# Moving the second rank's weight loads, its split and the first rank's stores behind the first units' turned rows, and ending the last table at the fifteenth step

## The chip, the cores and the metric

The kernel runs on one core of a Trainium2 chip. The metric is the device time in microseconds (us) of one execution. Engines are named as in the profile: PE (matrix multiply), DVE (vector), ACT (scalar), POOL (GpSimd, which here issues the indirect DMAs) and SP (which issues most of the other DMAs).

## The reference

The first part is an attention in which columns, not tokens, are normalised: for each of 4 batches a 256x256 matrix `softmax(kn^T qn)` is formed from 5056 tokens and applied to `v`. The second part is a top-1 mixture of 8 experts over all 20224 rows of its result:

```
logits = x @ w_gate;  e_idx = argmax(logits);  gate_w = softmax(logits)[e_idx]
eom = sigmoid(x @ w_output_gate)
for e in range(8):
    mask = e_idx == e
    h = maximum(x[mask] @ w1[e], 0)        # 256 -> 1024
    ye = h @ w2[e]                         # 1024 -> 256
    out[mask] = gate_w[mask] * eom[mask, e] * ye
```

## The kernel before, in words

The attention of each batch is a gram stage (`gram`), a softmax and a mix (`mix`). While a batch is mixed, its tokens are routed: each token's row is scattered to a slot of its expert in DRAM (`xs_d`) by indirect DMAs of POOL, eight for each group of 1024 tokens (L731). After the last group two more indirect DMAs fill the slots behind the last token of each region (L772).

The expert part works in units of 256 tokens of one expert (`blocks`). Experts are ordered by the number of their tokens; the place in this order is the rank. For a unit, its rows are read from `xs_d` into `xg` (L1013), scaled and cut into two f16 halves `xr` by ACT (L1065) and DVE (L1066), and turned by two pairs of DMA transposes into `xt` (L1070, issued by SP; two instructions to a unit). `h_part` runs four times a unit, each time 12 matmuls (L1091 to L1093) into a PSUM tile that ACT (L1095) and DVE (L1096) turn into the halves of `hb`. `y_part` multiplies `hb` by the second weights (L1117 on the high half, L1119 on the low one) and ACT (L1125) and DVE (L1126) write `yo`, which POOL scatters to the output (L1132). u0, u1, ... below are these units in order.

Weights. For each rank the raw weights come in two halves (the first and the second matrix). `load_raw` reads them on SP: for the second rank in two pieces each into `vall`, a buffer of the attention (L339), for later ranks in one 1 MB transfer into `raw` (L341). `split` squares them on ACT for a scale (L404), sums that by a small matmul (L410), and cuts them into f16 halves on ACT (L431) and DVE (L432). `keep` stores the halves to the scratch `wsc` in DRAM (L439); the first rank's `keep` calls are put into a list `held` instead, two of them with two 512 KB stores each. Units u0 to u6 use the first rank's halves where they lie in `wbuf`; from u7 on POOL fetches each unit's weights from `wsc` (L984).

Two checkpoints make tables: the early one covers the first ten units, the last one (`final`, L792 to L882 on DVE) all others. POOL reads a mark behind the scatters (L744), and the indices of later units wait for it.

What sets the order: `_beside` advances one generator and feeds others at a rate: `run` yields the expert work step by step, `preps` the weight work (`prep`), `tail` the last steps of the last mix. `pause(n)` yields n times. Each engine executes its instructions in the order that results, after a scheduler that keeps program order among dependent work and has some freedom elsewhere; `behind("SP")` puts a DMA behind the last main instruction of SP. SP issues its DMAs in order, and an SP instruction that waits (a transpose for its `xr`, say) holds all that follow on SP.

Of the kernel before, what the change touches and what calls it, by code (L numbers as in the profile page):

```python
# [26 lines left out]
def _beside(main, *others):  # L27

    due = [0.0 for _ in others]
    for _ in main:  # L30
        for i, (gen, rate) in enumerate(others):
            due[i] += rate
            while due[i] >= 1.0:
                due[i] -= 1.0
                next(gen, None)
# [3 lines left out]
def tile_colnorm_attention_then_top1_moe(  # L39
# [57 lines left out]
    for u in range(NUNIT):  # L97
# [6 lines left out]
        else:  # L104
            pair, half = divmod(u - MID, 2)
# [46 lines left out]
    PRATE = 1  # L152
    ALONE = 18
    LATE = 12
    MWAIT = 12
    BRATE = 0.7
    SOON, SRATE = 20, 1.0
    WRATE = 0.45
    WAITW = 1
    RWAIT = 3  # L160
    PIECES = "0 0 01 00 0 1 01 1 00"
    PWAIT = 2
    SMALL = 9
    VAFTER = 6
    AHEADW = 2
# [99 lines left out]
    @contextmanager  # L265
    def behind(*engines):
        with ExitStack() as held_back:
            for e in engines:
                if e in last:
                    held_back.enter_context(tc.issue_after(last[e]))  # L270
            yield

    def in_turn(gen, *engines):
        while True:
            with behind(*engines):
                try:
                    next(gen)
                except StopIteration:
                    return
            yield  # L280

    def pause(n):
        for _ in range(n):
            yield
# [38 lines left out]
    def load_raw(r, half, tag):  # L323
        if tag == "v":
            raw = [v_rows() for i in range(2)]
        else:
            if tag == "st":
                raw = wk.tile([P, R, CW], F32, tag="st", name=f"raw{r}_{half}", bufs=STB)
            else:
                raw = wide(f"raw{r}_{half}")  # L330
            whole = raw.rearrange("p r w -> p (r w)")[:, :HW1]
            raw = [whole[:, i * HW1 // 2 : (i + 1) * HW1 // 2] for i in range(2)]
        row = nc.values_load(
            ri[0:1, r : r + 1], engines=[mybir.EngineType.SP], min_val=0, max_val=(E - 1) * P,
            skip_runtime_bounds_check_because="rows of the weights of an expert",
        )
        if tag == "v":
            for i, a in enumerate(raw):
                nc.sync.dma_start(a, wraw[half][bass.ds(row, P), i * HW1 // 2 : (i + 1) * HW1 // 2])  # L339
        else:  # L340
            nc.sync.dma_start(whole, wraw[half][bass.ds(row, P), :])  # L341
        return raw

    held = []
    parts_of = {}

    def prep(first, end, tag):
        todo = []
        for r in range(first, end):
            for half in range(2):  # L350
                with behind("SP"):
                    raw = load_raw(r, half, "v" if r == first else tag)
                todo.append(lambda raw=raw, half=half, r=r: in_turn(split(raw, half, r), "ACT", "DVE", "PE"))
                yield
                if len(todo) > AHEADW:
                    if r == first + 1:
                        yield from pause(PWAIT)
                    yield from todo.pop(0)()
        for f in todo:
            yield from f()  # L360
# [3 lines left out]
    def prep_first():  # L364

        raws = []
        for half in range(2):
            raws.append(load_raw(0, half, "raw"))
            yield
        yield from pause(RWAIT)  # L370
        parts = [in_turn(split(raw, half, 0), "ACT", "DVE", "PE") for half, raw in enumerate(raws)]
        for step in PIECES.split():
            for half in step:
                next(parts[int(half)], None)
            yield
        first_done.append(0)
        while not mixed:
            yield
        for part in parts:
            yield from part  # L380
# [215 lines left out]
    def finish(gen):  # L596
        for _ in gen or ():
            pass
# [544 lines left out]
    def blocks(a, z):  # L1143

        got = dict.fromkeys(("x", "prep"), a)
        todo = sorted(range(max(a, FIRST[1]), z), key=lambda u: (asked_at(u), u))

        def adv(stage, step, n):
            for u in range(got[stage], min(n, len(units), z)):
                step(u)  # L1150
                got[stage] = u + 1

        g = a
        while g <= z:
            while g < z and g + 1 > len(units):
                yield
            while todo and asked_at(todo[0]) <= g:
                u = todo.pop(0)
                assert u < len(units)
                fetch_w(0, u)  # L1160
                fetch_w(1, u)
            adv("x", fetch_x, got["prep"] + XAHEAD - (got["x"] in BY_POOL))
            if g > a + 1:
                store(g - 2)
            if g == a:
                yield
            if g == 0:
                yield
            adv("prep", prepare, g + 1)
            if g == 0:  # L1170
                yield from pause(XWAIT)
            if g < z:
                hb = wide("hb").rearrange("p r w -> p (r w)")[:, :HW1]
                units[g]["h"] = hb.bitcast(F16).rearrange("p (a f m) -> p a f m", a=2, f=FC)
            for fp, steps in enumerate(ORDER):
                for kind, part in steps:
                    if kind == "h" and g < z:
                        h_part(g, part)
                    if kind == "y" and g > a:
                        y_part(g - 1, part)  # L1180
                adv("prep", prepare, min(g + 1 + XP, got["prep"] + (fp % 2 or g == a)))
                yield
            g += 1
        store(z - 1)
# [12 lines left out]
    run = blocks(0, NUNIT - TAIL)  # L1197
# [4 lines left out]
    preps = prep_first()  # L1202
    tail = mix(B - 1)
    for i in range(ALONE):
# [5 lines left out]
        for _ in range(PRATE):  # L1210
            next(preps, None)
    mixed.append(True)
    rest, preps = preps, prep(1, E, "st")
    for _ in range(AHEADW):
        next(preps)
    _beside((next(tail) for _ in range(2)), (run, BRATE), (rest, 1))
    finish(rest)
    finish(early)
    _beside(tail, (run, BRATE))
    for keep in held:  # L1220
        keep()
    final = checkpoint(True)
    next(final)
    _beside((next(run) for _ in range(MWAIT)), (preps, SRATE))
    finish(final)
    _beside((next(run) for _ in range(SOON - MWAIT)), (preps, SRATE))
    _beside(run, (preps, WRATE))
# [38 lines left out]
```

## Time and profile before

| what | value |
|---|---|
| median of 3 runs | 1264.32 us (1263.8 to 1269.23) |
| profiled execution | 1267.87 us, span 1266.2 us |
| mean granted PE clock of that execution | 0.975 |
| PE busy | 1194.1 us (94% of the span) |
| DVE, ACT, POOL busy | 767.9, 619.9, 566.5 us |

The profiled execution is one single execution; its time is its span and 1.67 us around it, and it lies 3.55 us above the median. All views below are of this execution. A timeline row gives the start, the time from start to end (for xN rows of the whole group), engine, line, operation, output and inputs, and in brackets how long the engine stood idle before it and what released it. PE rows overlap: a matmul of 256 columns lasts 0.27 us but the next one starts 0.11 us later at the full clock.

### The profile page before, as it was taken

How to read it: one execution, taken by the hardware profiler on the slowest of the kernel's cores; microseconds unless marked ns; L12 is line 12 of the kernel's file. 1: busy time of each engine (PE TensorE's matmuls, PEld its weight loads, DVE VectorE, ACT ScalarE, POOL GpSimd, SP SyncE). 2: the span in 40 equal slices, each digit the busy share in tenths (PEclk: the TensorE clock that was granted, in tenths of full speed). 3: DMA queues.
4: the chain of work that ended last, by engine and by line, in shares of the span. 5: the costliest groups of instructions: out<-in, count | busy, mean ns of one | idle time of the engine just before them, and what ended most of it. 6: DMA issues, size and time to landing. Idle time of an engine off the chain costs nothing. (4 is left out here: it accounts for less than half of the span.)

```text
span 1266.2 us, 25393 instructions
## 1 busy us (share of the span) xinstructions
PE 1194.1 (94%) x9138; PEld 950.0 (75%) x9138; DVE 767.9 (61%) x2292; ACT 619.9 (49%) x1233; POOL 566.5 (45%) x561
## 2 busy tenths in 40 slices
PE   9999899997748799999999999999999999999997
PEld 8888888897746477777777777777777777777775
DVE  7667547554546767575767666755555655555552
ACT  6577448545544365555555455543333333333442
POOL 0003653654445424445454544454445554444442
PEclk9999999898878999999999999999999999999999
DMA  9976776654537998465556554983334533347852
GB/s 324 329 245 222 235 242 224 233 182 154 191 124 178 239 276 221 136 146 142 144 148 142 145 140 111 247 186 70 73 71 136 143 73 78 78 114 209 193 178 62
DMA packets 175161, 214.68 MB, mean 170 GB/s; under 512 B 120200, under 2 KB 123790, under 8 KB 169528
## 3 DMA queue, kind: packets, MB, share of 16 engines
q1 hardware_dynamic: 130600, 126.58, 36.7%
q0 software_dynamic: 43312, 86.01, 23.7%
q8 instruction: 74, 1.21, 0.4%
q14 instruction: 55, 0.45, 0.2%
q10 hardware_dynamic: 1120, 0.42, 0.1%
HBM read 275.55 MB, written 61.41 MB: 266 GB/s over the span
## 5 line engine op out<-in xcount | busy, mean ns | idle before, releaser
L1096 DVE SCALAR_TENSOR_TENSOR hb<-h_ps,hb 128x512 f16<-128x512 f32 (+1 forms) x360 | 226.2, 634 | 239.3 <-ACT hb L1095 183.6
L1095 ACT ACTIVATE hb<-h_ps 128x512 f16<-128x512 f32 (+1 forms) x360 | 194.7, 549 | 274.6 <-PE h_ps L1093 177.9
L1132 POOL DMA_INDIRECT out_dram<-yo,b_id x162 | 168.2, 1038 | 244.3 <-DVE p2e L294 143.8
L731 POOL DMA_INDIRECT xs_d<-st,r_si x160 | 167.8, 1049 | 239.1 <-ACT st L656 150.5
L1117 PE MATMUL y_ps<-wbuf,hb 128*128 128x512 f16 x784 | 266.4, 380 | 1.3 <-DVE yo L1126 0.6
L1091 PE MATMUL h_ps<-xt,wbuf 128*128 128x256 f16 (+1 forms) x928 | 227.8, 258 | 4.8 <-DMA xt<-xr 3.2
L1092 PE MATMUL h_ps<-xt,wbuf 128*128 128x256 f16 (+1 forms) x928 | 227.8, 258 | 1.5 <-issue 1.5
L1093 PE MATMUL h_ps<-xt,wbuf 128*128 128x256 f16 (+1 forms) x928 | 227.6, 257 | 1.0 <-issue 1.0
L1119 PE MATMUL y_ps<-wbuf,hb 128*128 128x256 f16 x784 | 213.1, 274 | 1.9 <-issue 0.9
L1117 PEld LDWEIGHTS <-hb 128*128 128x128 f16 x1296 | 126.8, 98 | 115.3 <-issue 1.9
L1117 PE MATMUL y_ps<-vall,hb 128*128 128x512 f16 x512 | 173.2, 379 | 1.4 <-issue 0.9
L505 PE MATMUL s_ps<-qk 128*128 128x256 f32 x640 | 150.1, 384 | 0.1
L1119 PEld LDWEIGHTS <-hb 128*128 128x128 f16 x1296 | 127.0, 98 | 26.7 <-issue 7.0
L1119 PE MATMUL y_ps<-vall,hb 128*128 128x256 f16 x512 | 139.6, 273 | 1.1 <-issue 0.8
L1091 PE MATMUL h_ps<-xt,vall 128*128 128x256 f16 x512 | 139.5, 272 | 0.7 <-issue 0.7
L1093 PE MATMUL h_ps<-xt,vall 128*128 128x256 f16 x512 | 139.5, 273 | 0.0
L1092 PE MATMUL h_ps<-xt,vall 128*128 128x256 f16 x512 | 139.5, 273 | 0.0
L653 PE MATMUL x_ps<-ah,vh 128*128 128x272 f32 x320 | 105.6, 332 | 32.2 <-ACT st L656 17.3
L984 POOL DMA_INDIRECT wbuf<-wsc,wi x102 | 107.3, 1052 | 57.6 <-PE h_ps L1093 26.3
L505 PEld LDWEIGHTS s_ps<-qk 128*128 128x128 f32 x640 | 118.9, 192 | 15.8 <-issue 1.4
L1065 ACT ACTIVATE xr<-xg,b_sx 128x256 f16<-128x256 f32 x162 | 74.3, 501 | 111.7 <-DVE b_sx L295 61.2
L1091 PEld LDWEIGHTS <-wbuf 128*128 128x128 f16 x928 | 91.3, 98 | 32.3 <-issue 6.0
(212 smaller groups left out, 2057.9 us busy)
## 6 DMA issues: line engine op xcount, KB each, us to landing
qk<-in_q_dram SPq DMA_DIRECT2D x75, 256.0 KB
qk<-in_k_dram SPq DMA_DIRECT2D x75, 256.0 KB
vall<-in_v_dram SPq DMA_DIRECT2D x32, 512.0 KB
raw<-in_moe_w_dram SPq DMA_DIRECT2D x14, 1024.0 KB
xg<-xs_d SPq DMA_DIRECT2D x30, 272.0 KB
wsc<-whi SPq DMA_DIRECT2D x14, 512.0 KB
wsc<-wlo SPq DMA_DIRECT2D x14, 512.0 KB
vall<-in_v_dram SPq DMA_DIRECT2D x8, 480.0 KB
```

The lines of the kernel that those rows point to most:

```text
L505: nc.tensor.matmul(s_ps[:, c, :], kt[:, 1, t, c * P : (c + 1) * P], qt[:, 0, t, :], start=st == 0 and t0 == 0 and t == 0 and c == 0 and n ...
L653: nc.tensor.matmul(x_ps[:, :CW], vh[:, c, tsl], ah[:, c, :], start=c == 0, stop=False)
L731: ins = nc.gpsimd.indirect_dma_start(out=xs_d[:, :], out_offset=bass.IndirectOffsetOnAxis(ap=si[:np_, t : t + 1], axis=0), in_=st[:np_, t, ...
L984: nc.gpsimd.indirect_dma_start(out=weight(half, u), out_offset=None, in_=wsc[half][:end, :], in_offset=bass.IndirectOffsetOnAxis(ap=units[ ...
L1091: nc.tensor.matmul(hp, w1s[:, 0, c, fs], xh, start=fi == 0 and c == 0, stop=False, **KWM)
L1092: nc.tensor.matmul(hp, w1s[:, 0, c, fs], xl, start=False, stop=False, **KWM)
L1093: main(PE=nc.tensor.matmul(hp, w1s[:, 1, c, fs], xh, start=False, stop=fin, **KWM))
L1095: main(ACT=nc.scalar.activation(hh, h_ps[:, :, :w], AF.Relu))
L1096: ins = nc.vector.scalar_tensor_tensor(out=hb[:, 1, 2 * fp : 2 * fp + 2, :w], in0=h_ps[:, :, :w], scalar=0.0, in1=hh, op0=ALU.max, op1=ALU ...
L1117: nc.tensor.matmul(y_ps, hb[:, 0, f, tsl], w2s[:, :, f, :], start=f == 0, stop=False, **KWM)
L1119: PE=nc.tensor.matmul(y_ps[:, 0, :], hb[:, 1, f, tsl], w2s[:, 0, f, :], start=False, stop=f == FC - 1, **KWM)
L1132: ins = nc.gpsimd.indirect_dma_start(out=out[:, :], out_offset=bass.IndirectOffsetOnAxis(ap=un["id"][:, t : t + 1], axis=0), in_=un["yo"][ ...
```

## The change

Four constants and two places of code. `MWAIT`, the number of `run` steps over which the last table's work is spread before it is finished, goes from 12 to 15. `PWAIT`, the pause before the second rank's first split, goes from 2 to 4, and that pause with the split stands ahead of the load of the third rank's first half instead of behind it. The two `next(preps)`, which issue the second rank's raw loads, stand behind the last steps of the mix instead of ahead of them. The first rank's stores are issued one pair after `KWAIT` = 6 steps of `run` and the other after 3 more, instead of both ahead of the last table.

```
-    MWAIT = 12
+    MWAIT = 15
...
-    PWAIT = 2
+    PWAIT = 4
+    KWAIT = 6
...
             for half in range(2):
+                if (r, half) == (first + 1, 0):
+                    yield from pause(PWAIT)
+                    yield from todo.pop(0)()
                 with behind("SP"):
                     raw = load_raw(r, half, "v" if r == first else tag)
...
                 if len(todo) > AHEADW:
-                    if r == first + 1:
-                        yield from pause(PWAIT)
                     yield from todo.pop(0)()
...
     rest, preps = preps, prep(1, E, "st")
-    for _ in range(AHEADW):
-        next(preps)
     _beside((next(tail) for _ in range(2)), (run, BRATE), (rest, 1))
     finish(rest)
     finish(early)
     _beside(tail, (run, BRATE))
-    for keep in held:
-        keep()
+    for _ in range(AHEADW):
+        next(preps)
     final = checkpoint(True)
     next(final)
-    _beside((next(run) for _ in range(MWAIT)), (preps, SRATE))
+    for n in (KWAIT, KWAIT // 2, MWAIT - KWAIT - KWAIT // 2):
+        _beside((next(run) for _ in range(n)), (preps, SRATE))
+        if held:
+            held.pop(0)()
     finish(final)
```

On SP, at the first units, the order before is this. `xr_4679` holds u2 and u3, `xr_5052` u4 and u5, `xr_5334` u6 (x4 is two units' transposes):

```order
237 L1070 DMA_TRANSPOSE xt<-xr_4679 128x4x128 x4
238 L439 DMA wsc_85<-wbuf_184 128x2048 x2
239 L439 DMA wsc_86<-wbuf_185 128x2048 x2
240 L1009 TENSOR_LOAD gi
241 L1013 ISA
242 L1013 DMA xg<-xs_d 128x544
243 L1009 TENSOR_LOAD gi
244 L1013 ISA
245 L1013 DMA xg<-xs_d 128x544
246 L333 TENSOR_LOAD ri
247 L341 ISA
248 L341 DMA raw_0_5009<-in_moe_w_dram 128x2048
```

```order
249 L1070 DMA_TRANSPOSE xt<-xr_5052 128x4x128 x4
250 L333 TENSOR_LOAD ri
251 L341 ISA
252 L341 DMA raw_1_5291<-in_moe_w_dram 128x2048
253 L439 DMA wsc_85<-whi 128x2048
254 L439 DMA wsc_85<-wlo 128x2048
255 L1070 DMA_TRANSPOSE xt<-xr_5334 128x4x128 x2
```

Of the changed kernel the same place on SP (its lines are two higher; `xr_5043` holds u4 and u5, `xr_5322` u6):

```order
244 L1072 DMA_TRANSPOSE xt<-xr_5043 128x4x128 x4
245 L441 DMA wsc_85<-wbuf_184 128x2048 x2
246 L441 DMA wsc_86<-wbuf_185 128x2048 x2
247 L1072 DMA_TRANSPOSE xt<-xr_5322 128x4x128 x2
248 L441 DMA wsc_85<-whi 128x2048
249 L441 DMA wsc_85<-wlo 128x2048
250 L334 TENSOR_LOAD ri
251 L342 ISA
252 L342 DMA raw_0_5332<-in_moe_w_dram 128x2048
253 L334 TENSOR_LOAD ri
254 L342 ISA
255 L342 DMA raw_1_5361<-in_moe_w_dram 128x2048
```

The first rank's four stores stand behind the transposes of u4 and u5 instead of ahead of them, and the third rank's two raw loads behind u6's transposes and the second rank's first two stores. Ahead of the rows shown the four loads to `vall` have moved from ahead of the transposes of u2 and u3 to behind them, and all four reads of `xg` stand between them and the transposes of u4.

On DVE, before, the last table's first long operations stand ahead of the first `hb` of u2 (the first L1096 here):

```order
666 L1066 SCALAR_TENSOR_TENSOR xr_5052<-xg,b_sx,xr_5052 128x256 x2
667 L828 TENSOR_TENSOR tb_pr<-tb_bm,ef 128x496
668 L828 TENSOR_TENSOR tb_pr<-tb_bm,tb_r_4888 128x496
669 L793 TENSOR_SCALAR tb_ni<-tb_n 128x8
670 L829 TENSOR_REDUCE tb_res<-tb_pr 128x62
671 L1096 SCALAR_TENSOR_TENSOR hb<-h_ps,hb 128x512
672 L829 TENSOR_REDUCE tb_res<-tb_pr 128x62
```

In the changed kernel they stand behind it (the first L1098 here):

```order
665 L1068 SCALAR_TENSOR_TENSOR xr_5043<-xg,b_sx,xr_5043 128x256
666 L794 TENSOR_TENSOR tb_n<-rcr,done 128x8
667 L807 TENSOR_TENSOR tb_r_4921<-done,eor 128x8
668 L1098 SCALAR_TENSOR_TENSOR hb<-h_ps,hb 128x512
669 L830 TENSOR_TENSOR tb_pr<-tb_bm,ef 128x496
670 L830 TENSOR_TENSOR tb_pr<-tb_bm,tb_r_4884 128x496
671 L795 TENSOR_SCALAR tb_ni<-tb_n 128x8
672 L1098 SCALAR_TENSOR_TENSOR hb<-h_ps,hb 128x512
```

Three operations of 496 columns (two L828, one L829) have moved behind the first `hb` of u2. On ACT one of the two squarings of the second rank's first half (L404) has moved in the same way. From about u9 on the two orders are alike but for small swaps, and the numbers of instructions are the same.

## Rows read from the trace of the kernel before

**Rows 1.** Busy time of the engines in four stretches of the span (length; then PE, PEld, DVE, ACT, POOL busy with instruction counts; the granted PE clock; the DMA engines' share; GB/s).

```profile
280.00:400.00 120.00, 84.74 (x616) 77.29 (x615) 60.23 (x259) 58.18 (x144) 60.44 (x62) 0.83 0.47 151
400.00:460.00 60.00, 50.21 (x348) 34.12 (x346) 42.59 (x164) 28.61 (x52) 23.53 (x23) 0.94 1.11 249
460.00:1266.20 806.20, 795.66 (x6509) 598.92 (x6506) 489.52 (x1468) 364.23 (x721) 382.49 (x368) 1.00 0.55 138
```

**Rows 2.** The same view by tens of us, at the stretches the prediction speaks of.

```profile
350.00:360.00 10.00, 1.96 (x11) 1.65 (x11) 1.43 (x8) 0.39 (x1) 7.22 (x8) 0.70 0.50 158
360.00:370.00 10.00, 2.49 (x11) 2.49 (x12) 2.17 (x6) 3.08 (x6) 3.48 (x4) 0.50 0.54 177
...
410.00:420.00 10.00, 6.78 (x42) 3.82 (x40) 6.41 (x25) 0.91 (x2) 8.01 (x7) 0.94 1.08 352
420.00:430.00 10.00, 8.65 (x50) 4.74 (x48) 6.69 (x33) 4.24 (x9) 4.25 (x5) 0.89 1.29 185
430.00:440.00 10.00, 7.98 (x66) 5.94 (x63) 9.68 (x33) 7.71 (x11) 0.15 (x1) 1.00 1.17 156
440.00:450.00 10.00, 8.27 (x53) 5.88 (x54) 6.38 (x20) 4.63 (x10) 2.55 (x3) 0.83 1.05 283
```

**Rows 3.** The waits of PE from 400 to 460 us (what waited for what: us in total, times, longest).

```profile
PE h_ps L1091 <- DMA xt<-xr: 2.8, 1, 2.8
PE h_ps L1091 <- issue: 1.6, 2, 1.1
PE h_ps L1092 <- issue: 1.5, 2, 1.2
PE y_ps L1119 <- DVE hb L1096: 0.8, 1, 0.8
PE y_ps L1117 <- DVE yo L1126: 0.6, 1, 0.6
```

**Rows 4.** PE's timeline around u4's first matmul.

```profile
438.56 0.38 PE L1117 MATMUL y_ps<-wbuf,hb 128*128 128x512 f16 x1
441.73 0.27 PE L1091 MATMUL h_ps<-xt,wbuf 128*128 128x256 f16 x1 [2.79 <-DMA xt<-xr]
441.83 0.27 PE L1092 MATMUL h_ps<-xt,wbuf 128*128 128x256 f16 x1
...
442.84 0.42 PE L1092 MATMUL h_ps<-xt,wbuf 128*128 128x256 f16 x1
443.06 0.42 PE L1093 MATMUL h_ps<-xt,wbuf 128*128 128x256 f16 x1
...
446.23 0.27 PE L1092 MATMUL h_ps<-xt,wbuf 128*128 128x256 f16 x1
```

**Rows 5.** SP's timeline of DMA issues.

```profile
400.03 0.70 SPq L339 DMA_DIRECT2D vall<-in_moe_w_dram  x1
...
403.44 5.85 SPq L1070 DMA_TRANSPOSE xt<-xr  x4
409.33 3.71 SPq L439 DMA_DIRECT2D wsc<-wbuf  x4
414.62 2.00 SPq L1013 DMA_DIRECT2D xg<-xs_d  x2
418.97 0.62 SPq L341 DMA_DIRECT2D raw<-in_moe_w_dram  x1
419.62 15.40 SPq L1070 DMA_TRANSPOSE xt<-xr  x4
435.79 0.35 SPq L341 DMA_DIRECT2D raw<-in_moe_w_dram  x1
...
445.29 2.52 SPq L1070 DMA_TRANSPOSE xt<-xr  x2
```

**Rows 6.** The queue that carries SP's DMAs, by packets, MB and share of 16 engines' time, from 405 to 410 us and then from 425 to 430 us.

```profile
q1 hardware_dynamic: 1791, 0.91, 133.2%
...
q1 hardware_dynamic: 264, 0.20, 106.6%
```

**Rows 7.** DVE's timeline at the rows the prediction speaks of.

```profile
414.40 0.66 DVE L828 TENSOR_TENSOR tb_pr<-tb_bm,ef 128x496 f32<-128x496 f32 x1
414.99 0.66 DVE L828 TENSOR_TENSOR tb_pr<-tb_bm,tb_r 128x496 f32<-128x496 f32 x1
...
415.94 0.67 DVE L829 TENSOR_REDUCE tb_res<-tb_pr 128x62 f32<-128x496 f32 x1 [0.20 <-DVE tb_ni L793]
...
423.31 0.69 DVE L1096 SCALAR_TENSOR_TENSOR hb<-h_ps,hb 128x512 f16<-128x512 f32 x1 [6.70 <-issue]
...
438.33 1.29 DVE L1096 SCALAR_TENSOR_TENSOR hb<-h_ps,hb 128x512 f16<-128x512 f32 x2
```

**Rows 8.** ACT's timeline at the rows the prediction speaks of.

```profile
408.39 1.05 ACT L404 ACTIVATE whi<-vall 128x1024 f16<-128x1024 f32 x1
...
422.68 0.60 ACT L1095 ACTIVATE hb<-h_ps 128x512 f16<-128x512 f32 x1 [11.16 <-PE h_ps L1093]
...
458.53 1.05 ACT L404 ACTIVATE whi<-raw 128x1024 f16<-128x1024 f32 x1
```

**Rows 9.** POOL's timeline: the large one of the two scatters that fill the slots behind the last tokens, and the mark.

```profile
420.74 0.97 POOL L772 DMA_INDIRECT xs_d<-st,tb_ei  x1 [0.30 <-issue]
...
440.84 0.58 POOL L744 DMA_DIRECT2D mark<-xs_d  x1 [10.68 <-issue]
```

## The prediction

> **What bounds the kernel now.** I read the busy times by stretches first. From 460 us to the end PE is busy for 795.66 of 806.2 us at full clock, and the change leaves the amount of its work alone; so the only place to win is ahead of that [rows 1]. From 400 to 460 us, where every moved instruction lies, PE is busy for 50.21 of 60 us: 9.79 us idle, and some busy time at a lower clock (0.94) [rows 1]. Nothing here can be won beyond those 9.79 us and what the clock costs.
>
> Then I looked where they lie. By tens of us PE is weakest from 410 to 420 (6.78) and then 430 to 450 (7.98 and 8.27) [rows 2]. PE's waits name three causes: one wait of 2.8 us for the turned rows of u4, several rows called "issue", 3.1 us of them on two of the h lines alone, and 1.4 us of waits for DVE [rows 3]. These are three different stalls.
>
> First, the turned rows. PE's last matmul before it starts at 438.56 and u4's first at 441.73 [rows 4]. SP issued u4's and u5's four transposes from 419.62 on, behind four stores of the first rank (409.33 to 413) and a 1 MB raw load (418.97) [rows 5]. Second, the "issue" stall: ACT sat idle for 11.16 us until 422.68, named as waiting for PE's h matmuls, and DVE 6.70 us until 423.31 [rows 7, 8], while PE crept. Third, DVE: it is busy for 9.68 of 10 us from 430 to 440 [rows 2], with the last table, the second rank's split and `hb` in one queue.
>
> **The change part by part.**
>
> The wait for u4's rows. SP's queue takes transposes slowly when other traffic is beside them: from 405 to 410 us its 1791 packets took 133.2% of 16 engines for 5 us, so 1.332 x 80 / 1791 = 0.06 us each; from 425 to 430 it got 264 packets through in 106.6%, 0.32 us each [rows 6]. In that second stretch the large scatter behind the last tokens, issued at 420.74, was under way; POOL's mark, which waits for the scatters, came only at 440.84 [rows 9]. In the changed order the raw loads to `vall` (2 MB) and four reads of `xg` stand ahead of u4's transposes, and the stores and the third rank's load no longer do. SP's time for that, from its rows: the transposes of u3 end at about 405.5; the four loads take some 5 us as they did up to 400.7; four reads of `xg` at 1.0 us each (2.00 for two) make 414.5 [rows 5]. So u4's transposes are issued at about 415 to 418, only 2 to 5 us earlier, but behind 3 MB that were started earlier and so with their packets ahead of the large scatter. I expect u4's rows by about 425. Then PE can start u4 when DVE has freed a PSUM tile: the pair of `hb` that starts at 438.33 takes 1.29 us, its first half ends at about 439.0 [rows 7]. Gain: 441.73 - 439.0 = 2.7 us. Bounds: 0, if the rows are still late, and 2.79, the whole wait.
>
> The Trainium skill ("DMA: Bandwidth & Descriptors", section on queues, rings and completion order) says that an SDMA engine alternates between the queue rows that have work, a packet at a time. The trace bears on it: the transposes crawled beside the scatter [rows 6, 9]. By this rule the order on SP alone would not free transposes that start while the scatter runs; u5's, which wait for DVE, will still crawl, but they have 15 us in hand.
>
> The clock. After the wait PE's matmuls ran from 442.84 to 446.23 at the lower of its two levels, 1.2 GHz (starts 0.22 us apart instead of 0.11) [rows 4]; the granted clock of 440 to 450 is 0.83 [rows 2]. At full clock those 3.39 us of work take 1.7. Shorter gaps, of 0.6 and 0.8 us, were not followed by such a fall [rows 3]. Gain: between 0 and 1.7; I take 1.7, since the wait that came before it is gone.
>
> What moves behind the stall on DVE and ACT. Two L828 and an L829, about 0.6 us from start to start each, ran at 414.40 to 416.6, while DVE had nothing else; in the changed order they stand behind `hb` of u2, which can't run before 423.3 [rows 7]. That is 1.9 us of DVE work pushed into its fullest stretch. On ACT one squaring of 1.05 us, run at 408.39, is pushed in the same way [rows 8]. PE waited for DVE for only 1.4 us in the whole stretch [rows 3], so part of a delay of DVE is taken up by work that PE still has: the cost lies between 0 and 1.9 + 1.0 = 2.9 us. I take 1.2, about two thirds of DVE's part; the last table ending at the fifteenth step gives the rest room.
>
> The "issue" stall from 413 to 423. It is under a run of POOL's indirect DMAs that the change leaves alone. The same picture stands at 350 to 370 us: PE busy for 1.96 and 2.49 of 10 us at a DMA share of 0.50 and 0.54 [rows 2], so the load of SP's queue isn't needed for it. I take no change. Bounds: 0, and about 7 us of gain if the stores were its cause.
>
> The stores and the third rank's raw loads, now later. Stores from about 431 on hold nobody up by themselves; the raw load is issued behind u6's transposes (445.29 to 447.8 in the rows) and the second rank's stores, so at about 449 instead of 418.97. ACT first reads it at 458.53 [rows 5, 8]. That leaves 9 us for 1 MB behind 1 MB of stores; at the 283 GB/s of 440 to 450 [rows 2] 2.1 MB take 7.4 us. It just fits. Cost 0 as my value, bounds 0 and 5 us (below). u7's transposes now follow 2 MB of raws but have some 20 us until u7.
>
> Sum, against the profiled execution: 1267.87 - 2.7 - 1.7 + 1.2 = 1264.7. That execution lies 3.55 us above the median, so on the median's scale: 1264.32 - 3.2 = 1261.1, say 1261.
>
> **The rivals.**
>
> A. DVE takes it all back. u4 is then no longer held by its rows but by `hb`, at 438.33 plus the 1.9 us moved, plus ACT's 1.0: PE starts u4 at about 442, as before, and the clock falls as before. Time 1264. For it: DVE's 9.68 of 10 us [rows 2]. Against it: part of the table work now runs later than that.
>
> B. The stores cause the stall of 413 to 423. They were issued just ahead of it, at 409.33 [rows 5]. Without them PE would run through: 3.2 + 7 = 10 us won, 1254. Against it: the stretch of 350 to 370 us.
>
> C. Slower: the third rank's raw load comes late. If DMA moves 156 GB/s, as from 430 to 440 [rows 2], the 2.1 MB take 13.5 us, and ACT stands at the squaring L404 until 462.5, 4 us late, with the `hb` activations of two units queued behind it; PE runs dry. The second half and the raws behind it press on u7's transposes and weights in the same way, another 4 us or so. 1264.3 - 3.2 + 8 = 1269, and with a clock fall or two on top 1272. It decides from a landing after 458.5 us on.
>
> D. The change doesn't do what it says: SP is held at a read of `xg` ahead of u4's transposes, which go out at 420 as before and crawl. Nothing is won, and the moved work costs its 1.2: 1265.5.
>
> **How the numbers follow.** My forecast 0.45, A 0.18, B 0.17, C 0.14, D 0.06. A measurement here can tell about 0.5% (6.3 us) from no change, so faster means below 1258.0 and slower above 1270.6. Faster: B, and a quarter of my own case, where the "issue" stall shrinks a little too: 0.17 + 0.12 = 0.29. Slower: the larger part of C, and a little of A and D: 0.12. Same: the other 0.59. The range goes from 1254 (B) to 1269 (C); my case's own is 1258 to 1264.
>
> **What would show it.** In the profile after: no wait of PE for `xt` of u4, and u4's first matmul at about 439 to 440; matmul starts 0.11 us apart from 442 to 446; ACT's idle time of about 11 us until 422.7 still there; the first `hb` of u2 on DVE still at about 423.3, with the two L830 behind it; DVE full from 424 to 442; the raw load at about 449 and no wait of ACT for it at L406. I am wrong if the 11 us shrink (B), if a wait for DVE of about 3 us stands where the wait for rows was (A), or if waits of ACT for `raw` or of PE for weights stand at 455 to 480 (C).

## The result, and the profile after

The changed kernel is slower, by about half a per cent: 1268.11 us median of 22 runs (1258.79 to 1281.65) against 1264.06 us of 22 runs of before (1256.07 to 1275.31), a ratio of 1.0058 with a 95% interval of 1.0036 to 1.0079. All ratios here are estimated from fast executions alone while medians and ranges are over all, so a ratio isn't the quotient of its two medians (1.0032 here), and e10, whose profiled execution took 3145.08 us, is used for its ratio and not for its profile. The profiled execution took 1268.14 us (span 1266.4 us, mean granted clock 0.976), close to the one of before (1267.87 us). So this pair of profiles doesn't show the loss as a whole: each is one execution out of a spread of some 20 us. The loss is found only with more executions of both, below.

Around the units the lines of the kernel after are two higher (L1091 of before is L1093, L1096 is L1098). The stretches of [rows 1], of the kernel after:

```profile
280.00:400.00 120.00, 88.98 (x654) 81.97 (x652) 62.61 (x267) 60.30 (x150) 64.31 (x65) 0.86 0.48 157
400.00:460.00 60.00, 54.52 (x390) 37.65 (x391) 45.92 (x173) 31.57 (x59) 23.28 (x22) 0.97 0.76 239
460.00:1266.40 806.40, 791.04 (x6443) 594.38 (x6440) 485.62 (x1452) 362.81 (x713) 379.26 (x366) 0.99 0.55 139
```

Where all moved instructions lie, PE is busier: 54.52 of 60 us against 50.21, at a clock of 0.97 against 0.94. But it is busier ahead of it too (88.98 against 84.74 of 120 us, where the two orders hardly differ), and behind it PE now idles for 15.4 us (806.40 - 791.04) where it idled for 10.5. By tens of us, against [rows 2]:

```profile
350.00:360.00 10.00, 5.52 (x44) 5.00 (x42) 4.25 (x15) 3.20 (x7) 7.64 (x8) 1.00 0.77 246
...
410.00:420.00 10.00, 6.79 (x34) 3.10 (x33) 3.38 (x9) 3.66 (x8) 6.22 (x7) 0.83 1.04 329
420.00:430.00 10.00, 10.00 (x77) 7.25 (x76) 9.20 (x54) 3.53 (x7) 2.52 (x3) 1.00 0.31 84
430.00:440.00 10.00, 8.85 (x70) 6.60 (x69) 9.69 (x19) 7.40 (x13) 1.97 (x2) 1.00 0.53 208
440.00:450.00 10.00, 9.79 (x73) 6.79 (x72) 6.62 (x28) 6.43 (x12) 2.34 (x3) 1.00 0.78 250
```

Of the three stalls of the prediction, the wait for u4's rows and the fall of the clock at 440 to 450 us are gone (0.83 became 1.00). The stall of 410 to 420 us is still there (6.79 us busy, 6.78 before). PE's waits from 400 to 460 us, as in [rows 3], have no row for `xt` any more:

```profile
PE h_ps L1094 <- issue: 1.4, 2, 0.8
PE y_ps L1119 <- issue: 1.0, 3, 0.5
PE h_ps L1093 <- remote: 0.6, 1, 0.6
PE y_ps L1121 <- DVE hb L1098: 0.6, 1, 0.6
PE h_ps L1093 <- DVE hb L1098: 0.6, 1, 0.6
```

PE's timeline shows u4's first matmul 8.8 us earlier than in [rows 4] (432.94 against 441.73; 3.7 us of that are u1's earlier start), held only by `hb`. Later, two longer waits stand where before had none over 0.9 us:

```profile
432.94 0.27 PE L1093 MATMUL h_ps<-xt,wbuf 128*128 128x256 f16 x1 [0.56 <-DVE hb L1098]
...
815.25 0.27 PE L1093 MATMUL h_ps<-xt,wbuf 128*128 128x256 f16 x1 [2.52 <-DMA xt<-xr]
...
830.38 0.37 PE L1093 MATMUL h_ps<-xt,wbuf 128*128 128x256 f16 x1 [3.07 <-DVE hb L1098]
```

ACT's timeline, against [rows 8]: the stall stands in two pieces, each ahead of an `hb`; the third rank's raw load is read with a wait of 0.71 us; and `xr` of u8 (the last row) waits for transposes:

```profile
412.02 0.60 ACT L1097 ACTIVATE hb<-h_ps 128x512 f16<-128x512 f32 x1 [4.90 <-PE y_ps L1121]
...
417.98 0.60 ACT L1097 ACTIVATE hb<-h_ps 128x512 f16<-128x512 f32 x1 [4.32 <-remote]
...
452.09 1.06 ACT L406 ACTIVATE whi<-raw 128x1024 f16<-128x1024 f32 x1 [0.71 <-DMA raw<-in_moe_w_dram]
...
458.88 0.91 ACT L1067 ACTIVATE xr<-xg,b_sx 128x256 f16<-128x256 f32 x2 [2.79 <-DMA xt<-xr]
```

Before, in [rows 8]'s execution, the same write of u8's `xr` came without a wait:

```profile
463.13 0.90 ACT L1065 ACTIVATE xr<-xg,b_sx 128x256 f16<-128x256 f32 x2
```

SP's timeline answers to [rows 5]: the first rank's stores (428.44) behind u5's transposes, u6's transposes, the second rank's first stores, the two 1 MB loads of the third rank, and u7's transposes right behind these.

```profile
428.44 3.21 SPq L441 DMA_DIRECT2D wsc<-wbuf  x4
440.17 2.50 SPq L1072 DMA_TRANSPOSE xt<-xr  x2
442.72 0.57 SPq L441 DMA_DIRECT2D wsc<-whi  x1
...
445.18 1.83 SPq L342 DMA_DIRECT2D raw<-in_moe_w_dram  x2
447.54 3.01 SPq L1072 DMA_TRANSPOSE xt<-xr  x2
```

Why ACT's write of u8's `xr` has to wait for u7's transposes: `xr` of two units lies in one buffer of the tag "sq", of which there are two, and the high half of the second matrix's split (`whi2`, L398 of before), made first for the second rank, takes one of them for good (L1058 of before for `xr16`). From u8 on, the pair u8 and u9 gets the buffer of u6 and u7, and ACT may write it only when the transposes of u7 have read it.

### The profile page after: what moved, and what is told of

It reads as the page before. It is cut to its first block, busy times and chain, and to the rows that moved or that the text cites. A ratio compares the mean times of both kernels' runs of the same rounds, so it can differ in the third digit from the quotient of the medians.

```text
span 1266.4 us, 25392 instructions
## 1 busy us (share of the span) xinstructions
PE 1196.8 (94%) x9138; PEld 950.3 (75%) x9138; DVE 769.1 (61%) x2292; ACT 622.0 (49%) x1233; POOL 568.4 (45%) x561
## 5 line engine op out<-in xcount | busy, mean ns | idle before, releaser
L1098 DVE SCALAR_TENSOR_TENSOR hb<-h_ps,hb 128x512 f16<-128x512 f32 (+1 forms) x360 | 226.2, 634 | 241.0 <-ACT hb L1097 190.5
L733 POOL DMA_INDIRECT xs_d<-st,r_si x160 | 171.3, 1070 | 229.1 <-ACT st L658 123.9
L1093 PE MATMUL h_ps<-xt,wbuf 128*128 128x256 f16 (+1 forms) x928 | 227.8, 258 | 7.3 <-DVE hb L1098 3.6
L1093 PE MATMUL h_ps<-xt,vall 128*128 128x256 f16 x512 | 139.5, 273 | 0.3 <-issue 0.3
L1093 PEld LDWEIGHTS <-wbuf 128*128 128x128 f16 x928 | 91.2, 98 | 33.1 <-issue 6.9
```

Source lines behind the costliest of these rows:

```text
L733: ins = nc.gpsimd.indirect_dma_start(out=xs_d[:, :], out_offset=bass.IndirectOffsetOnAxis(ap=si[:np_, t : t + 1], axis=0), in_=st[:np_, t, ...
L1093: nc.tensor.matmul(hp, w1s[:, 0, c, fs], xh, start=fi == 0 and c == 0, stop=False, **KWM)
L1098: ins = nc.vector.scalar_tensor_tensor(out=hb[:, 1, 2 * fp : 2 * fp + 2, :w], in0=h_ps[:, :, :w], scalar=0.0, in1=hh, op0=ALU.max, op1=ALU ...
```

## The experiments

All kernels compute the reference in full. The experiments ran on five chips; on three of them before takes 1260 to 1271 us, on two 1196 to 1198 us (at a mean granted clock of 0.99 to 1.0 in the profiles, 0.97 to 0.98 on the others). Ratios are to before on the same chip, with 95% intervals.

**Each kernel again, and the parts (first chip).** e1 is the kernel after and e2 the kernel before, without an edit.

> The changed kernel once more, unchanged, for a second profile and second timing. Theory 1 (the gain ahead of 470 us is real, and the loss at u38 to u44, about 10.8 us at 812 to 832 us, is a chance event of that one execution): u1 to u6 again 4 to 6 us shorter than in the kernel before, and no stall of more than 1 us behind 480 us. Theory 2 (the loss belongs to the change, through the times at which DMAs meet): two stalls of 2 to 3 us with a lower clock stand again near u38 to u44.

> The kernel before once more, unchanged, for a second profile: how much of the difference of two profiles is between executions of one kernel. Theory 1: stalls like those at u38 to u44 show here too in some place, and the ratio is 1.000 within 0.002. Theory 2: no stall of over 1 us behind 480 us.

e3 moves only the stores, with `MWAIT` left at 12:

```
-    for keep in held:
-        keep()
...
+    for n in (KWAIT, KWAIT // 2, MWAIT - KWAIT - KWAIT // 2):
+        _beside((next(run) for _ in range(n)), (preps, SRATE))
+        if held:
+            held.pop(0)()
```

> Only the first rank's stores moved (6 steps, 3 more, 12 in all). My prediction's theory (the stores and the raw load ahead of u4's transposes make the wait of 2.8 us): that wait goes, 2 to 4 us faster. Rival (the wait is made by the large scatter alone): the wait stays, 0. Rival 2 (the later stores meet later transfers): slower by 3 us or more.

e4 has the two `next(preps)` behind the tail and the split with its pause ahead of the third rank's load, but not the stores, and `MWAIT` 12:

```
-    PWAIT = 2
+    PWAIT = 4
...
+                if (r, half) == (first + 1, 0):
+                    yield from pause(PWAIT)
+                    yield from todo.pop(0)()
...
-    for _ in range(AHEADW):
-        next(preps)
...
+    for _ in range(AHEADW):
+        next(preps)
     final = checkpoint(True)
```

> Only the weight side moved: the second rank's raw loads behind the last steps of the mix, the pause and the split ahead of the third rank's load. If the loss of the changed kernel belongs to the third rank's loads and weights coming later (my rival C): slower by 4 us or more, with waits for raw or for weights from 455 us on. If to DVE's moved table work (my rival A): slower by 0 to 3 us with waits for DVE from 424 to 442. If to neither: within 1 us.

Measured: e1 1268.36 us, 1.0033 (0.9998 to 1.0067), so here the change itself isn't told from before; e2 1261.59, 1.0019 (0.9980 to 1.0057), so the same kernel against itself gives no difference; e3 1263.82, 1.0027 (0.9991 to 1.0063), not resolved; e4 1269.19, 1.0063 (1.0029 to 1.0098). The loss is there without the stores. Theory 1 of e1 held in its first half (63.0 us from u1 to u6) and as to the late stall: u38 to u44 took 62.7 us, as before, and not 73.2 as in the first profile of after. And e2's profile, the second of the kernel before, has no wait for u4's rows at all and no row of 430 to 450 us below full busy time. PE's waits there, from 395 to 460 us:

```profile
PE y_ps L1117 <- ACT hb L1095: 3.8, 1, 3.8
PE h_ps L1091 <- issue: 0.9, 2, 0.5
PE h_ps L1092 <- issue: 0.5, 1, 0.5
PE h_ps L1093 <- issue: 0.3, 1, 0.3
```

So the first two gains of the prediction were read from a stall that another execution of the same kernel doesn't have.

**Loads and split apart (second chip).** e5 is the first half of e4, only the two `next(preps)` moved; e6 the second half, only `PWAIT` 4 and the split ahead of the third rank's load; e7 and e8 are the kernels after and before once more.

```
-    for _ in range(AHEADW):
-        next(preps)
     _beside((next(tail) for _ in range(2)), (run, BRATE), (rest, 1))
...
+    for _ in range(AHEADW):
+        next(preps)
     final = checkpoint(True)
```

> Only the second rank's raw loads moved behind the last steps of the mix; the pause stays 2 and the split behind the third rank's load. If the loss of the weight side (run e4: ratio 1.006) comes from the later loads: slower by about 0.5%, and the time from u1's start to u10's start is 104 to 111 us with waits for fetched weights. If it comes from the moved split: within 0.2% of before.

```
-    PWAIT = 2
+    PWAIT = 4
...
+                if (r, half) == (first + 1, 0):
+                    yield from pause(PWAIT)
+                    yield from todo.pop(0)()
...
-                    if r == first + 1:
-                        yield from pause(PWAIT)
```

> Only the pause of 4 and the first split ahead of the third rank's first load. If the loss comes from the split: slower by about 0.5%, with the second rank's stores about 10 us later than before and a wait for fetched weights at u7 to u9. If it comes from the later loads: within 0.2% of before.

> The changed kernel unchanged, a third profile. Theory (the change wins 4 to 6 us from u1 to u6 and gives 3 to 5 back at u6 to u10, where the second rank's weights are fetched later): u1 to u6 62 to 64 us, u6 to u10 41 to 45 us. Rival (the loss lies behind u12 as in the first profile, about 10 us at u38 to u44): u12 to u88 721 to 724 us instead of 711 to 716.

> The kernel before unchanged, a third profile. Theory (the wait of 2.8 us for u4's rows in the first profile was no fixed part of the kernel before, since the second profile has none): u1 to u6 61 to 65 us and no wait for the rows of u4. Rival (it is fixed): u1 to u6 about 68 us with a wait of 2 to 3 us for the rows of u4.

Measured: e5 1190.48 us, 0.9941 (0.9914 to 0.9969), faster; e6 1201.09, 1.0044 (1.0006 to 1.0081), slower; e7 1204.35, 1.0068 (1.0032 to 1.0103); e8 1194.29, 1.0001 (0.9966 to 1.0036). The us expected of e7 and e8 were missed: e7 took 57.3 us from u1 to u6 and 52.2 from u6 to u10, e8 58.5 to u6, with a wait of 0.67 us for u4's rows. The change has a part that wins and a part that loses, and the split's place is the one that loses. e7's profile shows it at its largest. SP's timeline of e7, then ACT's, then PE's waits from 392.7 us (u6's start) to 423.8 (u8's):

```profile
375.01 2.10 SPq L342 DMA_DIRECT2D raw<-in_moe_w_dram  x2
379.55 2.94 SPq L1072 DMA_TRANSPOSE xt<-xr  x2
...
405.97 5.03 SPq L1072 DMA_TRANSPOSE xt<-xr  x2
```

```profile
388.03 0.60 ACT L1097 ACTIVATE hb<-h_ps 128x512 f16<-128x512 f32 x1 [0.85 <-PE h_ps L1095]
404.88 0.91 ACT L1067 ACTIVATE xr<-xg,b_sx 128x256 f16<-128x256 f32 x2 [16.25 <-DMA xt<-xr]
405.69 0.45 ACT L1127 ACTIVATE yo<-y_ps,b_gs 128x256 f32<-128x256 f32 x1
407.05 2.33 ACT L433 ACTIVATE whi<-raw,wsw 128x512 f16<-128x512 f32 x2 [0.90 <-DVE invw L313]
409.28 1.06 ACT L1097 ACTIVATE hb<-h_ps 128x512 f16<-128x512 f32 x2
```

```profile
PE h_ps L1093 <- DVE r2e L306: 9.7, 1, 9.7
PE h_ps L1093 <- DVE hb L1098: 0.8, 1, 0.8
```

The 2 MB of raws are issued at 375, u7's transposes at 379.55, and not before 404.88 may ACT write u8's `xr`. Behind that write stand `yo`, the split and the evictions of u7 on ACT, and DVE's own half of `xr`; both engines do nothing from 390 to 400 us. PE runs out of free PSUM and waits 9.7 us: `h_ps` shares its PSUM tiles with the small sum `w_ps`, which DVE's r2e reads, and r2e stands on DVE behind the half of `xr` that waited for ACT.

**Take the wait away by another buffer, and undo the split (third chip).** e9 is the kernel after with `xr` of u8 and u9 in a free slot of the pool of the raw weights:

```
+            if u == 8:
+                spare = wk.tile([P, R, CW], F32, tag="st", name="xr16s", bufs=STB)
+                both = spare.rearrange("p r w -> p (r w)")[:, : 4 * C].bitcast(F16)
...
+            else:
+                both = wk.tile([P, 2, 2, C], F32, tag="sq", name="xr16").bitcast(F16)
```

> The changed kernel with one edit: the turned-row halves of u8 and u9 get a buffer of their own (a slot of the raw weights' pool), so that ACT's writing of them no longer waits for the transposes of u6 and u7 to have read theirs. Theory (the loss is this wait: u7's transposes stand behind the third rank's 2 MB on SP's queue and land late, and ACT with all its evictions waits for the buffer): ACT's wait of 5 to 16 us before the halves of u8 goes, PE's wait of 2 to 10 us at u6 to u7 goes, and the time is 0.4 to 0.8% shorter than the changed kernel's. Rival (the third rank's raw rows themselves, or the fetched weights, are late): PE's wait stays, under another name, and the time stays 0.5% above before.

e10 is the kernel after without the split's part (stores, loads and `MWAIT` 15 are left in):

```
-    PWAIT = 4
+    PWAIT = 2
...
-                if (r, half) == (first + 1, 0):
-                    yield from pause(PWAIT)
-                    yield from todo.pop(0)()
...
+                    if r == first + 1:
+                        yield from pause(PWAIT)
```

> The changed kernel without its pause and split part: the third rank's first load stands again ahead of the first split, pause 2; loads, stores and the fifteenth step as changed. Theory (the split part alone makes the loss): the time is 0.4 to 0.8% below before, as with the loads alone. Rival (stores or the fifteenth step carry a part of the loss): at or above before.

e11 is e5 again, e12 is e5 with e9's buffer.

> The loads alone once more. Theory (the later loads give the gain that I had put on u4's rows): 0.3 to 0.8% below before again. Rival (the gain of run e5 was one of chance): within 0.2%.

> The loads alone and the buffer for u8 and u9. Theory (without the split part ACT doesn't wait for that buffer): same as the loads alone within 0.2%, 0.3 to 0.8% below before. Rival (the buffer is a gain by itself): clearly below the loads alone.

Measured: e9 1200.85 us, 1.0039 (1.0009 to 1.0068); e10 1196.29, 0.9980 (0.9944 to 1.0015); e11 1190.17, 0.9962 (0.9936 to 0.9989); e12 1188.97, 0.9951 (0.9915 to 0.9988). Without the split's part no loss is seen (e10), but not the gain of the loads alone either; what the stores and the fifteenth step cost is not resolved, and the fifteenth step was not tried alone. With the other buffer the wait is gone, but e9 is still slower than before: 1.0039, where the kernel after gave 1.0058, 1.0033 and 1.0068, so that a gain of the buffer isn't shown either. The rival of e9 came nearer. In e9's profile ACT writes u8's `xr` with a wait of 0.99 us, and not for transposes. From u6's start to u8's (393.0 to 409.8) PE's waits are these:

```profile
PE h_ps L1098 <- DMA xt<-xr: 0.5, 1, 0.5
PE h_ps L1098 <- DMA xt<-xr16s: 0.3, 1, 0.3
```

But from u8's start to u10's (409.8 to 437.4) a wait for the weights that POOL fetches from `wsc` has come:

```profile
PE y_ps L1124 <- DMA wbuf<-wsc,wi: 4.1, 1, 4.1
PE h_ps L1098 <- DMA xt<-xr16s: 0.3, 1, 0.3
```

**Take the raws out of SP's queue, and other places of the split (fourth chip).** e13 is the kernel after with the third rank's two raw loads issued by ACT, e14 by POOL; their place in the program stays, but these queues reach it earlier (in e13 at 404 and 428 us, in e14 at 396.5 and 426.2), so two things change at once, the queue and the time. The register with the row's place is read by the new issuer as well (not shown).

```
-            nc.sync.dma_start(whole, wraw[half][bass.ds(row, P), :])
+            (nc.scalar if r == 2 else nc.sync).dma_start(whole, wraw[half][bass.ds(row, P), :])
```

> The changed kernel with the third rank's two raw loads issued by ACT, where the order lets them go out some 40 us earlier and not on SP's queue; SP's stores and transposes as changed. Theory (the 2 MB on SP's queue right ahead of u7's transposes make them late): no wait of ACT of 5 us or more before the halves of u8, no wait of PE of 2 us or more at u6 to u7, 0.4 to 0.8% shorter than the changed kernel. Rival (the later stores of the second rank and the later split are enough): the waits stay and the time stays 0.5% above before.

> The same with POOL as the issuer, between its scatters. Theory: as in run e13, less what two more issues cost POOL. Rival: as in run e13.

e15 is the kernel after with the third rank's first load three steps later:

```
                     yield from todo.pop(0)()
+                    yield from pause(3)
                 with behind("SP"):
```

> The changed kernel with three more empty steps ahead of the third rank's first load: on SP one of its 1 MB loads stands behind u7's transposes instead of ahead. Theory (bytes ahead of the transposes set their landing): the wait of ACT before u8's halves is 3 to 8 us, about half of 10 to 16. Rival: unchanged or longer, since the third rank comes later still.

e16 is e6 with the pause left as it was:

```
-    PWAIT = 4
+    PWAIT = 2
```

> The split ahead of the third rank's load as in run e6, but with the pause of 2 of before: the loads stand ahead of u6's transposes instead of u7's. Theory: the late transposes are those of u6, of which PE and the buffer of u8 are less in need, so the loss is smaller than e6's 0.4%: 0 to 0.3%. Rival (the split's place itself costs): 0.4% again.

Measured: e13 1268.53 us, 1.0044 (1.0012 to 1.0076); e14 1268.22, 1.0043 (1.0010 to 1.0076); e15 1269.91, 1.0075 (1.0050 to 1.0100); e16 1273.03, 1.0075 (1.0037 to 1.0113). None of the four is told from the kernel after, and all are slower than before. e13 does take ACT's wait away (its timeline at u8):

```profile
463.60 0.91 ACT L1067 ACTIVATE xr<-xg,b_sx 128x256 f16<-128x256 f32 x2 [1.04 <-issue]
```

and again the fetched weights come late in its place. PE's waits of e13 from u6's start to u8's (468.3 to 493.2):

```profile
PE h_ps L1093 <- DMA wbuf<-wsc,wi: 4.6, 1, 4.6
PE y_ps L1119 <- DMA wbuf<-wsc,wi: 1.9, 1, 1.9
```

In e15 the wait of u8's `xr` is still 4.16 us, in e16 6.75 us: neither three steps more for the raws nor a shorter pause lets the transposes land in time. e15's wait is what its theory said; e16's theory failed, its loss is 0.75% and not 0 to 0.3%. In e16 the 2 MB were issued at 438.30, ahead of u6's transposes, and u7's followed only at 456.25: the wait doesn't need the raws right ahead of u7's. e16 also shows that the split's place loses without the longer pause.

**The parts that were left, on one more chip.** e17 is e5 and e18 is e10, unchanged.

> The loads alone a third time. Theory (they are the change's gain): 0.3 to 0.7% below before, and from u1 to u12 115 to 119 us where the profile isn't disturbed. Rival: within 0.2%.

> The changed kernel without its pause and split part, once more, for a profile that isn't disturbed. Theory (the split part makes the loss): no wait of ACT of more than 2 us for the buffer of u8's halves, no wait of PE of 2 us or more at u6 to u7, time at or below before. Rival: those waits stand there too.

Measured: e17 1270.57 us, 0.9989 (0.9956 to 1.0023); e18 1269.73, 1.0027 (0.9992 to 1.0062). On this chip neither is told from no change. e18 had no wait of ACT at u8 and none of PE from u6 to u8, as its theory said, and the 115 to 119 us expected of e17 were 125.8. The loads' gain of the two faster chips isn't confirmed on a slower one.

**All profiles side by side.** From PE's timelines I read the first matmul of u1, u6, u8 and u10 in every profile but e10's; the table has the us between them, and ACT's idle time ahead of u8's `xr` (T: ended by transposes, as the profile names it; in e4 and e6 it names "issue", and elsewhere DVE or nothing; a dash is none).

```
                                 u1-u6  u6-u8  u8-u10   ACT at u8
split where it was
  before, e2, e8                  68.8   16.4   20.9    -
                                  61.0   19.8   22.6    0.93 T
                                  58.5   20.3   22.2    1.88
  e3 (stores)                     64.5   20.6   23.8    4.32 T
  e5, e11, e17 (loads)            58.2   21.5   17.9    0.86
                                  58.1   19.5   17.9    0.87
                                  67.5   19.5   17.9    -
  e12 (loads, buffer)             57.6   19.5   17.9    -
  e18 (all but the split)         64.2   21.8   17.9    -
  mean                            62.0   19.9   19.9
split ahead of the third rank
  after, e1, e7                   63.2   17.1   21.3    2.79 T
                                  63.0   20.4   23.2    4.93 T
                                  57.3   31.1   21.1    16.25 T
  e4 (no stores)                  63.1   25.7   22.4    10.10
  e6 (split alone)                60.7   25.3   20.9    10.05
  e15, e16                        60.7   20.0   24.9    4.16 T
                                  61.7   33.1   17.6    6.75 T
  mean                            61.4   24.7   21.6
split ahead, wait taken away
  e9 (buffer)                     56.6   16.8   27.6    0.99
  e13, e14 (raws off SP)          68.6   24.9   19.9    1.04
                                  64.4   21.3   17.6    1.04
  mean                            63.2   21.0   21.7
```

From u1 to u6, where the prediction saw its gain, the means don't differ (62.0 against 61.4). But the groups mix chips: on the slower chips alone, five profiles each, they are 65.2 and 62.3, with single rows from 60.7 to 68.8, so a gain of some us there is neither shown nor excluded.

From u6 to u10 the new place of the split costs 6.5 us on average (24.7 + 21.6 against 19.9 + 19.9), 0.5% of the time, which is about the size of the loss; on the slower chips alone it is 4.9 (45.1 against 40.2). Only the sum of the two columns compares all rows, since with the loads' part PE does more work ahead of u8's first matmul. The stretch u6 to u8 of before, then of e11, both without any idle time of PE:

```profile
468.60:485.00 16.40, 16.40 (x136) 12.97 (x135) 13.96 (x38) 12.28 (x21) 7.19 (x7) 1.00 0.95 261
```

```profile
393.30:412.80 19.50, 19.50 (x155) 14.79 (x153) 15.75 (x41) 13.41 (x22) 10.59 (x10) 1.00 1.08 303
```

The sums also show where the loads' part gains. Without any stall, u6 to u10 takes 37.3 us (before). With the split where it was, the four profiles without the loads' part take 37.3, 42.4, 42.5 and 44.4 us, where PE waits 0, 3.2, 3.7 and 4.0 us for the weights of u8; the five with it take 39.4, 37.4, 37.4, 37.4 and 39.7, with waits of 1.9, 0, 0, 0 and 2.1. So in these profiles what the loads' part saves lies at u8's weights and not at u4's rows; why the weights come earlier then was not tried.

ACT's wait at u8 is over 2.7 us in all seven profiles of the second group and in one of nine of the first, e3. In five of the seven the profile names the transposes; in e4 and e6 the DMA packets show them too: u7's transposes are 1024 packets of 256 bytes, and the last of them ends 1.5 and 2.6 us ahead of ACT's write, against 0.9 to 1.5 us in the five others. Without the wait 2.9 us are left of the 6.5 (21.0 + 21.7 against 39.8), on three profiles only, with fetched weights waited for in all three (4.1 us in e9, 6.5 in e13, 2.0 in e14).

## Why the prediction was wrong

The forecast was 1261 us; the median is 1268.11. It lies in the stated range, but on the other side of before: the sum had 4.4 us of gains that the runs as a whole don't show, and a cost that it put at 0.

**Wait for u4's rows, -2.7 us: the mechanism was right, the worth was not.** The wait went as foretold, and u4 started on `hb` (its transposes went out at 408.99 us, earlier than the 415 to 418 forecast). But of the three profiles of before only the first has the wait at 2.79 us; e8 has 0.67 us and e2 none. From u1 to u4 before takes 41.9, 35.8 and 30.0 us (first profile, e2, e8), after 36.9, 36.7 and 27.7 (first profile, e1, e7).

**Clock, -1.7 us: the same.** After has 1.00 from 420 to 450 us, but e2 has 1.00 from 430 on too. The fall followed a wait that not every execution has.

**DVE, +1.2 us, and rival A: not seen.** DVE is full as foretold (9.20 and 9.69 us of two tens), yet PE's two longest waits for it in 400 to 460 us are 0.6 us each. In e4, u4's first matmul does wait 2.50 us for DVE (`wlo` of the second rank's split), so the term isn't nothing in every execution; it is not where the loss lies.

**The "issue" stall, 0: held.** The stores went, the stall of 410 to 420 us stayed (6.79 us busy; 7.05 in e3, where only the stores moved), so rival B (stores as its cause) falls. Its form was missed: the forecast had the first `hb` of u2 on DVE at 423.3 and ACT idle until 422.7; the first `hb` came at 412.65, and ACT's idle time in two pieces that ended at 412.02 and 417.98. e2, of before, has it in pieces too.

**Stores and third rank's raws, later: 0. This is the step that failed.** Its words were "u7's transposes now follow 2 MB of raws but have some 20 us until u7." That counts to the reader of `xt`, PE. The nearer user is the next writer of the transposes' source: ACT writes u8's `xr` into the buffer they read, 9 to 15 us after u7's own in the profiles where nothing holds it. In the seven profiles with the split ahead they land later, and ACT stands with the evictions and the split queued behind it, 2.79 to 16.25 us. The term was put at 0 with bounds 0 and 5; u6 to u10 measured 6.5 us more. In the first profile of after that stretch is 459 to 498 us, behind the 400 to 460 us in which the prediction looked for gains and costs. e9 and e13 bear on the wait from two sides: another buffer, or the raws out of SP's queue and, in e13, some 40 and 20 us earlier, and the wait for transposes at u8 is gone. That the raws alone make the transposes late is not shown: e3 waits 4.32 us with the split where it was, and e16 6.75 us with the raws 18 us ahead of u7's.

**Rival C** had the right neighbourhood, "raws behind it press on u7's transposes and weights in the same way", and the right side; but it put half of its price, 4 of 8 us, and its deciding sign on a wait of ACT for the raw load at L406, which measured 0.71 us. That its 1269 lies next to the 1268.11 measured is luck in part. D is out: u4's rows were in time.

What is shown: the loss is in the split's place (e4, e6 and e16 are slower; without it e10 isn't, and e18 not by more than its interval), the wait of ACT at u8 comes with it, and taking the wait away alone doesn't give the time back (e9, e13, e14). That the later half of the second rank (its stores and split come later too, so what POOL fetches is there later) makes up the rest is what the waits for `wbuf` suggest; it was not tried by itself, and such waits of 3.2, 3.7 and 4.0 us stand in e2, e8 and e3 as well. So how the remaining loss divides stays open. Open too is the jam of after near 815 to 830 us, far from any moved instruction, where the orders are alike: from u20 to u60 after took 416.9 us and e9 417.5, the others 405 to 410. Two of ten profiles with the split ahead have it in full and none of nine without, which is too few to tell chance from cause.

## What to carry to other kernels

A stall that one profile shows is worth its price only if other executions of the same kernel have it; where a kernel's runs differ by 20 us, read the same stretch in several profiles before its removal enters a sum. Profiles of different chips, or of orders that do different work between the same two marks, don't compare as they stand. When a large transfer goes ahead of a small one in a queue, look not only for who reads what the small one writes, but for who next writes what it reads: that user may be much nearer, and what stands behind it on its engine pays. Time the parts of a change apart: here moving the loads alone won 0.4 to 0.6% on two chips (0.9941, 0.9962, not told from nothing on a third with 0.9989), while the split's place lost about as much.

## What the hardware showed that was not expected

The same program took 1196 to 1198 us on two chips and 1260 to 1271 us on the others. In the profiles of before the mean granted clock was 0.997 against 0.975 and 0.976, 2% apart, while the times are 5% apart. Most of the difference lies ahead of the units: u1 starts at 334 us in e8 and at 395 to 400 us in the two profiles of before on the other chips, while from u10 to the end they take 755 against 760 to 762 us.

DMA engines can be full and move little. In e7 from 390 to 400 us, while ACT and DVE stood, the DMA share was 1.06 at 113 GB/s; in e8 (before, the same chip) in the same stretch 1.12 at 331 GB/s. The stretch of e7, then its queues by packets, MB and share of 16 engines:

```profile
390.00:400.00 10.00, 7.07 (x56) 5.30 (x55) 0.00 (x0) 0.00 (x0) 0.00 (x0) 1.00 1.06 113
```

```profile
q0 software_dynamic: 130, 0.94, 64.6%
q1 hardware_dynamic: 651, 0.19, 41.8%
```

And the queues of e8:

```profile
q1 hardware_dynamic: 1540, 2.62, 91.3%
q0 software_dynamic: 154, 0.68, 20.5%
```

A packet of POOL's indirect DMAs took 0.646 x 160 / 130 = 0.80 us in e7 and 0.205 x 160 / 154 = 0.21 us in e8; those of e7 were larger (7.2 KB on average against 4.4 KB), which alone doesn't make a ratio of nearly 4. At the same time a packet of the hardware queue took 0.10 us in both but carried 0.3 KB against 1.7 KB. So u7's transposes, in small packets, crawled beside fetches whose packets took long. The rule of the Trainium skill that the prediction named ("DMA: Bandwidth & Descriptors", section on queues, rings and completion order: an engine alternates between the rows that have work, a packet at a time) agrees with this: a queue of small packets beside one of slow packets gets few bytes through. No run here separates that from other causes, or shows that the page's packet is what the profile counts as one.
